# Unread products on TensorE in the planned gaps of the first two batches of a fused attention and FFN kernel

## The chip, the cores and the metric

The kernel runs on one core of a Trainium2 chip. The metric is the time of one execution on the device in microseconds (us), lower is better. The engines are named as in the profile: PE is TensorE (the matrix products; PEld its weight loads), DVE is VectorE, ACT is ScalarE, POOL is GpSimd, SP issues DMAs.

## The reference

Attention with a threshold on the scores is followed by a two-layer FFN. Each of 8 batches has 8 heads of 576 tokens by 64:

```python
scores = (1 / sqrt(64)) * q @ k.T
thresh = max(scores, axis=-1) - tau
scores = where(scores >= thresh, scores, -1e9)
attn = exp(scores - max(scores)); attn = attn / (sum(attn) + 1e-9)
x = (attn @ v)              # heads side by side: 4608 x 512
h = x @ w_in                # 512 x 2048
g = where(h >= 1, h, where(h <= -1, 0, (h + 1)**2 / 4))
out = g @ w_out             # 2048 x 512
```

## The kernel before, in words

Every large operand is split in a high and a low float16 part, so a product of two matrices is two or three products on PE. Heads go in pairs. A score tile is 128 queries by 576 keys of one head; its scores lie in one of two PSUM buffers, `s_ps[0]` and `s_ps[1]` (`s0` and `s1` of the pool `s`; in listings of the program `s_61` and `s_62`, in the profile both are `s`). Each buffer is two banks of 512 float32 columns, and the scores fill columns 0 to 287 of each bank.

A score tile goes through the engines like this: PE makes the scores (L806); DVE takes the row's maximum (L817 to L819); ACT takes the exponential (L822); DVE masks it and sums the row (L826, it reads the scores once more), then forms the divisor (L830, L831); POOL scales (L834), ACT makes the high part (L839), POOL the low part (L842), and a DMA transposes both (L845). PE multiplies by v (L924), ACT and DVE evict to x (L932, L936). The FFN's first product is L1000, its activation L1006 to L1023 on ACT and DVE, its second product L1049, the eviction L1068.

The first 130 us hold, beside the first batches, the preparation of the two weight matrices: they are loaded in 32 pieces, brought to float32 (L612 or L614, L621, L626, L630), measured by PE with `gram` (L637), scaled, and split (L682, L690, or PE's difference L702 and L703 with its eviction L709). v of the first batch is turned on PE (L526) in the buffers of the pool `s`.

No order is written by hand. `Plan.op` records each step with its engine, a cost in us, a key, what it comes after, and the buffers that it takes. `Plan.order` then plays the program through: each engine that is free takes the ready step of the lowest key, and the steps are emitted in the order in which they were started there; `o.t` is a step's start in the plan's own time. The keys are sums of tile numbers and fractions such as 19.77, 8.47 and 1.88. Every engine executes its steps strictly in the order emitted. Semaphore waits are put in from the tiles that the emitted instructions write and read.

## Time and profile before

| | us |
|---|---|
| median of 3 runs (1160.36 to 1167.64) | 1161.93 |
| profiled execution, its own time | 1162.28 |
| span in the profile | 1160.3 |
| PE busy | 1096.6 |
| DVE busy | 944.1 |
| ACT busy | 901.7 |
| POOL busy | 801.2 |

The profiled execution lies 0.35 us above the median, and 2.0 us of it lie outside the span. A row of a timeline begins with its start and its duration in us; then come engine, line, operation, result and operands, shape and count; in brackets stands how long the engine had been idle, and what released it. A row of the stretches (windows) has, for each engine, its busy us and its number of instructions, then the granted TensorE clock as a share of full speed.

### The profile page before, as it was taken

To read this page: it belongs to the slowest core of one execution; us is meant where nothing else is said; L and a number is where in the kernel's file an instruction comes from. 1 tells how busy PE (TensorE), PEld (TensorE's weight loads), DVE (VectorE), ACT (ScalarE), POOL (GpSimd) and SP (SyncE) were. 2 spreads that over 40 slices of the span, in tenths; PEclk is the share of its full clock that TensorE was granted. 3 is DMA by queue.
4 is the path that set the end of the run, shared out by engine and by line. 5 is a ranking of instruction groups with operands and counts; after the bars stand their busy time and mean duration, and the time that the engine had idled before them with its cause. 6 is when DMAs were issued, how large, how long until landed. Compare 5 with 4: busy or idle time off the path is not lost.

```text
span 1160.3 us, 27210 instructions
## 1 busy us (share of the span) xinstructions
PE 1096.6 (95%) x9423; PEld 755.4 (65%) x9423; DVE 944.1 (81%) x2982; ACT 901.7 (78%) x1692; POOL 801.2 (69%) x957
## 2 busy tenths in 40 slices
PE   5767989899999999999999999999999999999998
PEld 3335656776677567676677676676677677676674
DVE  5899778989889988888889987898889889786241
ACT  6998877887798779877878788877888788686362
POOL 3578997776976787667966887667966887654000
PEclk8889999999999999999999999999999999999999
DMA  8797999679995799668795899669995898555000
GB/s 328 287 228 138 160 208 193 123 156 172 181 175 108 138 196 212 126 114 189 171 180 92 169 205 185 137 105 196 175 179 101 165 186 166 99 102 92 19 2 28
DMA packets 435929, 179.40 MB, mean 155 GB/s; under 512 B 400464, under 2 KB 407632, under 8 KB 435792
## 3 DMA queue, kind: packets, MB, share of 16 engines
q1 hardware_dynamic: 435792, 177.67, 75.4%
q8 instruction: 74, 1.21, 0.4%
q14 instruction: 63, 0.52, 0.1%
HBM read 45.09 MB, written 9.44 MB: 47 GB/s over the span
## 4 chain that ended last, share of the span: by engine, by line
PE 48%; DVE 22%; POOL 10%; ACT 7%; issue 7%; DMA 5%; SPq 1%; ACTq 0%; POOLq 0%; DVEq 0%
PE acc L1049 18%; PE ph L1000 17%; PE s L806 6%; PE ph L924 5%; DVE sm L817 5%; DVE e L826 4%; POOL hl L842 3%; POOL e L834 2%; DVE ph L1013 2%; ACT e L822 2%; DMA eT<-hl 2%; ACT hl L839 2%; DVE vb L499 1%; POOL raw L415 1%; DVE sm L818 1%
## 5 line engine op out<-in xcount | busy, mean ns | idle before, releaser
L842 POOL TENSOR_TENSOR hl<-e,hl 128x576 f16<-128x576 f32 x286 | 368.1, 1292 | 121.2 <-ACT hl L839 118.8
L1000 PE MATMUL ph<-x,WI 128*128 128x256 f16 (+1 forms) x4032 | 402.1, 257 | 1.0 <-DVE x L936 0.5
L1000 PEld LDWEIGHTS <-WI 128*128 128x128 f16 x4032 | 347.1, 98 | 55.7 <-issue 4.1
L834 POOL TENSOR_SCALAR e<-e,sm 128x576 f32<-128x576 f32 x286 | 221.4, 779 | 98.8 <-DVE sm L831 63.9
L822 ACT ACTIVATE e<-s,sm,pc 128x576 f32<-128x576 f32 x288 | 237.3, 832 | 51.9 <-DVE sm L818 33.1
L826 DVE SCALAR_TENSOR_TENSOR e<-s,sm,e 128x576 f32<-128x576 f32 x288 | 231.1, 812 | 43.6 <-ACT e L822 39.2
L839 ACT ACTIVATE hl<-e 128x576 f16<-128x576 f32 x286 | 194.5, 683 | 64.2 <-POOL e L834 58.0
L817 DVE TENSOR_REDUCE sm<-s 128x1 f32<-128x576 f32 x288 | 215.5, 748 | 31.5 <-PE s L806 30.7
L1049 PE MATMUL acc<-WO,ga 128*128 128x512 f16 x864 | 206.7, 379 | 0.8 <-ACT ob L1068 0.8
L806 PE MATMUL s<-kk,qq 128*128 128x288 f16 (+3 forms) x1360 | 181.3, 290 | 16.9 <-DVE e L826 15.2
L806 PEld LDWEIGHTS <-qq 128*128 128x128 f16 (+3 forms) x1360 | 106.8, 100 | 78.5 <-issue 42.3
L1013 DVE SCALAR_TENSOR_TENSOR ph<-ph,fcs,asq 128x512 f32<-128x512 f32 (+1 forms) x160 | 111.8, 699 | 45.7 <-ACT asq L1009 44.7
L1006 ACT ACTIVATE asq<-ph,fcs 128x512 f32<-128x512 f32 (+1 forms) x160 | 116.2, 738 | 38.6 <-PE ph L1000 37.8
L1049 PEld LDWEIGHTS <-ga 128*128 128x128 f16 x864 | 81.9, 98 | 83.6 <-issue 4.7
L924 PE MATMUL ph<-eT,vst 128*64 128x320 f16 (+2 forms) x1928 | 126.5, 284 | 6.9 <-DVE gb L1023 3.1
L924 PEld LDWEIGHTS <-vst 128*64 128x64 f16 x1928 | 101.4, 111 | 30.4 <-issue 19.3
L1018 ACT ACTIVATE ga<-ph,fcs 128x256 f16<-128x256 f32 (+1 forms) x160 | 70.5, 451 | 33.5 <-DVE ph L1013 31.0
L1009 ACT ACTIVATE asq<-asq 128x512 f32<-128x512 f32 x144 | 90.8, 630 | 2.3
L1023 DVE SCALAR_TENSOR_TENSOR ga<-ph,fcs,ga 128x256 f16<-128x256 f32 (+1 forms) x160 | 70.8, 451 | 25.0 <-ACT gb L1018 9.4
L1049 PE MATMUL acc<-WO,gb 128*128 128x512 f16 x306 | 73.3, 379 | 0.0
L428 POOL TENSOR_TENSOR nat<-raw,nat 128x576 f16<-128x576 f32 x56 | 71.4, 1283 | 2.5 <-ACT nat L421 2.4
L818 DVE TENSOR_SCALAR sm<-sm,pc 128x1 f32<-128x1 f32 x288 | 61.7, 214 | 10.5
(162 smaller groups left out, 1210.2 us busy)
## 6 DMA issues: line engine op xcount, KB each, us to landing
kk<-nat SPq DMA_DIRECT2D x112, 144.0 KB, 3.3
raw<-in_v_dram SPq DMA_DIRECT2D x32, 288.0 KB, 3.7
raw<-in_q_dram SPq DMA_DIRECT2D x32, 288.0 KB, 3.6
raw<-in_k_dram SPq DMA_DIRECT2D x32, 288.0 KB, 3.6
WO<-in_moe_w_in_dram SPq DMA_DIRECT2D x16, 512.0 KB, 7.7
out_dram<-ob SPq DMA_DIRECT2D x32, 256.0 KB, 2.6
qq<-nat SPq DMA_DIRECT2D x112, 72.0 KB, 2.1
x<-in_moe_w_out_dram SPq DMA_DIRECT2D x10, 512.0 KB, 5.6
```

Of the source, the lines that this page charges most:

```text
L806: T.matmul(ap(x, s_ps)[r, f, :SH], q, k, start=ql == kl == 0, stop=kl == 1)
L817: V.tensor_reduce(t[:, 0:1], sv(), AX.XY, ALU.max, negate=True)
L822: A.activation(halves(ap(e, es)[:, :S]), sv(), AF.Exp, bias=ap(m, sm)[:, 1:2], scale=ap(cb, pc)[:, 24 + v : 25 + v])
L826: V.scalar_tensor_tensor(halves(ap(e, es)[:, :S]), sv(), t[:, 2:3], halves(ap(e, es)[:, :S]), ALU.is_ge, ALU.mult, accum_out=t[:, 3:4])
L834: G.tensor_scalar(ap(e, es)[:, :S], ap(e, es)[:, :S], ap(m, sm)[:, 5:6], 1.0, ALU.mult, ALU.mult)
L839: A.activation(ap(x, hl)[:, :S], ap(e, es)[:, :S], AF.Copy)
L842: G.tensor_tensor(ap(x, hl)[:, w : w + S], ap(e, es)[:, :S], ap(x, hl)[:, :S], ALU.subtract)
L924: T.matmul(o[hd * D : (hd + 1) * D, :n], vt[:, k, hd * D : (hd + 1) * D], t[:, kb, hd * n : (hd + 1) * n], start=m == 0, stop=m == len(blo ...
L1000: T.matmul(h[:, i], WTh["i"][:, u, wl * 512 + c * P : wl * 512 + (c + 1) * P], x[:, cc, xl, c0 : c0 + n].rearrange("p (t n) -> p t n", n=P ...
L1006: A.activation(tv()[:, :, c], hv()[:, :, c], AF.Relu, bias=fcs[:, b, 2, q : q + 1], scale=fcs[:, b, 1, q : q + 1])
L1013: V.scalar_tensor_tensor(hv()[:, :, c], hv()[:, :, c], fcs[:, b, 0, q : q + 1], tv()[:, :, c], ALU.max, ALU.min)
L1049: T.matmul(ap(ab, accs), gv(h, gl)[:, x], WTh["o"][:, fc + i, wl * 512 : (wl + 1) * 512], start=fc + i == 0 and m == 0, stop=fc + i == NFC ...
```

## The change

It has two parts.

**Unread products.** Where the steps are emitted, a PE step whose planned start lies over 0.8 us behind the planned end of the PE step before it, and before 240 us of the plan's time, gets products put just ahead of it: 0.65 of the planned gap, at 0.056 us for each product. Each is 128x128 by 128x128 of the constant `ones` (bfloat16), with a weight load of its own, and writes columns 384 to 511 of the second bank of `s_ps[0]`, which nothing reads. There are 593 of them in 27 groups, of 9 to 53 products. The first group stands ahead of everything else on PE.

**Keys.** Keys pass through `plan.key`, which adds nothing while `SHIFT` is empty, and are rounded to 3 decimals. Ties between sums of fractions then fall differently. The order of all real steps is the same as before up to the place that the trace of before has at about 366 us, and differs from there to the end.

```diff
+SHIFT = {}
+FILL = (0.8, 240, 0.65)
...
+    def key(self, kind, i, key):
+
+        return key + SHIFT.get(kind, {}).get(i, 0)
...
-        o = Op(eng, cost, key, fn, work)
+        o = Op(eng, cost, round(key, 3), fn, work)
...
+    def keep_warm(us):
+
+        for _ in range(int(us / 0.056)):
+            T.matmul(s_ps[0][:, 1, 512 - P :], ones, ones, start=True, stop=True)
+
     with tc.manual_schedule():
+        free = 5.0
         for o in plan.order():
+            if o.eng == "PE":
+                if FILL[0] < o.t - free and o.t < FILL[1]:
+                    keep_warm(FILL[2] * (o.t - free))
+                free = o.t + o.cost
             o.fn()
```

The other lines of the diff put `plan.key(...)` around keys that were passed bare.

First place: PE, where a piece of w_in is split (`dgw` is its scale, `ph` a PSUM buffer), in the trace of before at 76.43 us. Before:

```order
L637 LDWEIGHTS WO
L637 MATMUL acc<-WO 128x128
L702 MATMUL ph_64<-WI,dgw_132 128x512 [waits DVE_49]
L703 LDWEIGHTS minus
L703 MATMUL ph_64<-WI,minus 128x512 [waits Pool_49]
L637 LDWEIGHTS WO [waits DMAHW2_49,DVE_49,Activation_49]
L637 MATMUL acc<-WO 128x128
```

And now (23 products at the first place, 18 at the second, of which the first of each is shown; L646 is the old L637, L712 the old L702):

```order
L646 LDWEIGHTS WO
L646 MATMUL acc<-WO 128x128
L1096 LDWEIGHTS ones
L1096 MATMUL s_61<-ones 128x128 [waits DVE_49]
...
L712 MATMUL ph_64<-WI,dgw_132 128x512
L713 LDWEIGHTS minus
L713 MATMUL ph_64<-WI,minus 128x512 [waits Pool_49]
L646 LDWEIGHTS WO [waits DMAHW2_49,Activation_49]
L646 MATMUL acc<-WO 128x128
...
L1096 LDWEIGHTS ones
L1096 MATMUL s_61<-ones 128x128
```

The step L702 did not move against its neighbours, but a group stands ahead of it whose first product waits for a DVE instruction: by the semaphore's value, the mask (old L826) that is the last reader of the buffer `s_61` ahead of it in the program.

Second place: PE ahead of an FFN product L1049 (now L1062), in the trace of before at 167.30 us. Before:

```order
L702 MATMUL ph_63<-WO,dgw_134 128x512
L703 LDWEIGHTS minus
L703 MATMUL ph_63<-WO,minus 128x512 [waits Pool_49]
L1049 LDWEIGHTS ga_111
L1049 MATMUL acc<-WO,ga_111 128x512
```

Now, with 19 products, the first of which is shown:

```order
L712 MATMUL ph_63<-WO,dgw_134 128x512 [waits DVE_49]
L713 LDWEIGHTS minus
L713 MATMUL ph_63<-WO,minus 128x512 [waits Pool_49]
L1096 LDWEIGHTS ones
L1096 MATMUL s_61<-ones 128x128 [waits Activation_49]
...
L1062 LDWEIGHTS ga_111
L1062 MATMUL acc<-WO,ga_111 128x512
```

The FFN product, which uses no scores, now stands behind a wait for ACT: the exponential (old L822) that reads `s_61`.

Third place: DVE where the order first differs by the rounded keys, in the trace of before at about 367 us (`sm` holds a tile's row statistics, `scs` the scale of v). Before:

```order
L826 SCALAR_TENSOR_TENSOR e_92,sm_125<-s_62,sm_125,e_92 128x576
L830 TENSOR_SCALAR sm_125<-sm_125 128x1
L831 RECIPROCAL sm_125<-sm_125 128x1
L826 SCALAR_TENSOR_TENSOR e_93,sm_126<-s_61,sm_126,e_93 128x576
L481 TENSOR_REDUCE scs<-ph_65 128x1
```

Now:

```order
L837 SCALAR_TENSOR_TENSOR e_92,sm_125<-s_62,sm_125,e_92 128x576
L490 TENSOR_REDUCE scs<-ph_65 128x1
L302 TENSOR_SCALAR scs<-scs 128x1
L303 TENSOR_SCALAR scs<-scs 128x1
L304 TENSOR_SCALAR scs<-scs 128x1
L492 TENSOR_SCALAR scs<-scs 128x1
L841 TENSOR_SCALAR sm_125<-sm_125 128x1
L842 RECIPROCAL sm_125<-sm_125 128x1
L837 SCALAR_TENSOR_TENSOR e_93,sm_126<-s_61,sm_126,e_93 128x576
```

The scale of v moved ahead of a tile's divisor and the next tile's mask.

## The prediction

> **What bounds the kernel now.** I read the page first, then stretches by granted clock, then the chain of waits and the timelines of PE, DVE and ACT up to 207 us, where the change does most of its work.

> ```profile
> span 1160.3 us, 27210 instructions
> ...
> PEclk8889999999999999999999999999999999999999
> ```

> The second line is the granted clock in tenths over 40 slices of 29 us: it is reduced in the first four only. The stretches tell the two regimes apart (columns: PE, PEld, DVE, ACT, POOL busy us; clock; DMA share; GB/s):

> ```profile
> 0.00:207.21 207.21, 157.92 (x1497) 100.99 (x1498) 168.69 (x558) 169.76 (x324) 157.88 (x235) 0.93 0.90 217
> 22.89:29.72 6.83, 5.95 (x30) 2.63 (x31) 6.58 (x19) 5.64 (x10) 3.83 (x5) 0.50 0.88 306
> 43.37:50.20 6.83, 5.90 (x24) 2.45 (x21) 4.90 (x15) 6.30 (x14) 4.85 (x13) 0.50 0.75 242
> 149.19:152.60 3.41, 3.41 (x30) 2.55 (x27) 1.29 (x6) 1.73 (x5) 3.25 (x10) 0.50 1.07 286
> 207.21:210.63 3.42, 3.00 (x28) 2.74 (x27) 3.42 (x6) 3.20 (x6) 3.42 (x4) 0.50 0.45 86
> 362.00:1100.00 738.00, 730.03 (x6149) 508.10 (x6147) 618.98 (x1956) 576.54 (x1079) 523.53 (x593) 1.00 0.76 147
> ```

> From 362 us on PE is busy 730.03 of 738 us: PE carries that part, at full clock. Up to 207 us PE is busy 76%, DVE and ACT 81 and 82%: there the engines wait for each other in turn, and whatever is late at the end of it moves the whole PE part behind it. So the change is worth what it does to the arrival at 207 us, plus what the new order does after about 366 us. In this first part PE has 49 us of idle time and some stretches at half clock.

> **The gain: products that run at half clock today and lie on the chain of waits.** There are four such places.

> ```profile
> 9.97 5.33 PE L526 MATMUL s<-dgw,raw 128*128 128x128 f32 x20 [1.55 <-POOL dgw L514]
> ...
> 16.06 2.93 PE L526 MATMUL s<-dgw,raw 128*128 128x128 f32 x20
> ...
> 44.71 2.01 PE L702 MATMUL ph<-WI,dgw 128*128 128x512 f32 x2
> ...
> 47.95 2.08 PE L702 MATMUL ph<-WI,dgw 128*128 128x512 f32 x2 [0.29 <-DVE pc L402]
> ...
> 85.75 1.07 PE L702 MATMUL ph<-WI,dgw 128*128 128x512 f32 x2
> ...
> 129.71 2.23 PE L924 MATMUL ph<-eT,vst 128*64 128x320 f16 x30
> ...
> 148.65 3.73 PE L924 MATMUL ph<-eT,vst 128*64 128x320 f16 x30 [1.45 <-DMA eT<-hl]
> ```

> (a) The first turn of v takes 5.33 us, the second 2.93: at most 2.4 to win. Behind it the chain goes through loads:

> ```profile
> 26.80 6.33 DMA WO<-in_moe_w_in_dram
> 33.15 6.84 DMA x<-in_moe_w_out_dram
> ```

> The DMA engines are 88% taken in the stretch 22.89 to 29.72, so only 0.12 of 6.83 us is free to start loads earlier. I take 0.8 and keep 2.4 as the end. (b) Two differences L702 at half clock cost 2.01 and 2.08 against 1.07: 1.95. The group of 10 products between them finds no idle time in the trace and costs its own length, 0.6 at the pitch below; 1.4 is left. (c) L924 at 148.65 takes 3.73 against 2.23: 1.5; the group ahead of it, 16 products long, starts only when a mask on DVE releases its buffer:

> ```profile
> 148.27 0.81 DVE L826 SCALAR_TENSOR_TENSOR e<-s,sm,e 128x576 f32<-128x576 f32 x1
> ```

> That is 149.08, and with 0.9 for the group L924 is 1.3 late. I take zero for both together. (d) The half clock from 207.21 has no group ahead of it: zero. Together 2.2 us; the whole list without any lateness would be 5.9.

> [...]

> **The cost: groups that start late.** A group runs at the pitch of products with a load each:

> ```profile
> 92.01 2.84 PE L1000 MATMUL ph<-x,WI 128*128 128x128 f16 x48
> ```

> 2.84 / 48 = 0.059 us. 593 of them are 35 us, less than the 49 us of idle time. But the groups can't start when PE falls idle. They write into the first scores buffer, so each one waits for the last reader of that buffer ahead of it in the program (front, first and second place), and the real step stands behind it on PE. Where the gap came from that same reader, the whole group is added; where it came from elsewhere, the group adds a wait as well. [...]

> I price five groups in their own time frames: mask or exponential end, plus group, against the start of the next real step, and then the reader of what PE delivers late. They add up, since an earlier delay moves both sides.

> ```profile
> 64.30 0.81 DVE L826 SCALAR_TENSOR_TENSOR e<-s,sm,e 128x576 f32<-128x576 f32 x1
> ...
> 67.47 0.75 DVE L817 TENSOR_REDUCE sm<-s 128x1 f32<-128x576 f32 x1
> ...
> 76.88 0.81 DVE L826 SCALAR_TENSOR_TENSOR e<-s,sm,e 128x576 f32<-128x576 f32 x1
> ...
> 81.94 0.75 DVE L817 TENSOR_REDUCE sm<-s 128x1 f32<-128x576 f32 x1
> ...
> 91.83 0.81 DVE L826 SCALAR_TENSOR_TENSOR e<-s,sm,e 128x576 f32<-128x576 f32 x1
> ...
> 96.59 0.74 DVE L817 TENSOR_REDUCE sm<-s 128x1 f32<-128x576 f32 x1
> ```

> ```profile
> 65.17 0.40 PE L806 MATMUL s<-kk,qq 64*128 64x288 f16 x1 [3.06 <-DVE e L826]
> ...
> 76.43 1.13 PE L702 MATMUL ph<-WI,dgw 128*128 128x512 f32 x2 [1.64 <-DVE x L936]
> ...
> 77.61 0.39 PE L637 MATMUL acc<-WO 128*128 128x128 bf16 x4
> ...
> 79.34 1.13 PE L702 MATMUL ph<-WI,dgw 128*128 128x512 f32 x2 [1.34 <-ACT WI L709]
> ...
> 80.61 0.91 PE L806 MATMUL s<-kk,qq 64*128 64x288 f16 x12
> ...
> 91.76 0.41 PE L637 MATMUL acc<-WO 128*128 128x128 bf16 x4 [1.87 <-DVE WO L626]
> ...
> 94.78 0.91 PE L806 MATMUL s<-kk,qq 64*128 64x288 f16 x12
> ```

> - 65.17, 42 products (2.48): the mask ends at 65.11, the group at 67.59, the twelve score products 0.91 later at 68.50; DVE wants them at 67.47. Late by 1.0.
> - 76.43, 23 products (1.36), and 79.34, 18 products (1.06): the mask ends at 77.69, so L702 starts at 79.05. The work from 76.43 to 78.00 takes 1.57, the second group 1.06, so the second L702 starts at 81.68, 2.3 late, and the scores of 80.61 end at 83.9; DVE wants them at 81.94. Late by 1.9.
> - 91.76, 26 products (1.53): mask end 92.64, group end 94.17, 2.4 late; the scores of 94.78 end at 98.1, DVE wants them at 96.59. Late by 1.5.

> ```profile
> 113.24 1.10 PE L702 MATMUL ph<-WO,dgw 128*128 128x512 f32 x2 [3.24 <-DVE ph L295]
> ...
> 167.30 1.46 PE L1049 MATMUL acc<-WO,ga 128*128 128x512 f16 x6
> ...
> 176.33 1.17 PE L806 MATMUL s<-kk,qq 128*128 128x288 f16 x8
> ```

> ```profile
> 113.68 0.81 DVE L826 SCALAR_TENSOR_TENSOR e<-s,sm,e 128x576 f32<-128x576 f32 x1
> ...
> 116.43 0.76 DVE L817 TENSOR_REDUCE sm<-s 128x1 f32<-128x576 f32 x1 [0.47 <-PE s L806]
> ...
> 177.68 0.74 DVE L817 TENSOR_REDUCE sm<-s 128x1 f32<-128x576 f32 x1
> ```

> ```profile
> 168.29 1.55 ACT L822 ACTIVATE e<-s,sm,pc 128x576 f32<-128x576 f32 x2
> ```

> - 113.24, 28 products (1.65): mask end 114.49, group end 116.14. Late by 2.9, and DVE waits for PE already at 116.43.
> - 167.30, 19 products (1.12): the exponentials end at 169.84, the group at 170.96, L1049 is 3.7 late. PE has no gap from there on, so the scores of 176.33 are 3.7 late too. The first four of the eight products (0.6) end at 180.6; DVE wants them at 177.68. Late by 2.9.

> The sum is 10.2 us. Four more groups behind 80 us (13, 17, 26 and 17 products, 4.3 us) are left out of it, some of their lateness will be hidden, and they go into the upper end. The remaining groups I cost at nothing: they fall into idle time that is long enough, or into the loads' time before 40 us; if that cover is gone, each costs its length. So the first part ends 10.2 - 2.2 = 8.0 us later.

> **The order from 366 us.** The same steps, other neighbours. PE idles 738 - 730.03 = 8.0 us there, so 8 us is the most that a better order can win; a worse one could lose as much again (an estimate: the idle time doubled). No row speaks for a side, so zero, with 8 either way.

> The sum: 1162.28 + 8.0 = 1170.3 for the profiled execution; it stands 0.35 above the median, so 1170.

> **Rivals.** *The clock wins (not slower).* PE's lateness falls into slack on DVE and ACT, and the groups clear the half-clock stretches. For it: 49 us of idle time on PE, and four slow products on the chain. Against it: DVE's rows at 67.47 and 81.94 follow without idle time. It gives 1161.9 - 5.9 = 1156, up to 1162 with part of the lateness. Half of PE's busy time in the stretches up to 152.60 (5.95, 5.90 and 3.41) would be 7.6 us, of which the chain has those 5.9. *The groups themselves run at half clock.* The two longest groups in the middle of this part have 42 products each, and the second of them follows an idle time of 3.06 us (row 65.17); at twice 0.059 both together cost 84 x 0.059 = 5.0 us more: 1175. *The new order is worse:* 8 us on top, 1178; or better by 8, 1162. *The change does nothing:* the groups are in the program, so this only remains as a balance of gain and cost; it is inside the first rival.

> **How the numbers follow.** My forecast, 1164 to 1176, has 0.43; the clock wins 0.20; groups at half clock 0.13; a worse order 0.15, a better one 0.09. Changes under 1%, 1150.3 to 1173.6, count as within. Slower by over 1%: the worse order, most of the half clock and a fifth of the forecast, 0.37. Faster by over 1% needs the whole clock gain and a good order at once: 0.04. Within: 0.59. For 8 in 10 the range goes from the clock's end, 1156, to the worse order with some of the unpriced groups, 1181.

> **What would show it.** The L526 at about 10 us at 2.9, and the L702 at 45 to 50 us at 1.1, would show the gain; weight loads and L637 around them tell how much the loads swallow. The step L1049 of 167.30 should come some 10 us later than before, directly behind a group that waits for ACT, and PE should reach full load around 215 instead of 207. If that step comes earlier than 167 the cost is wrong. PE's idle time from there to 1100 us tells the new order: 8 us as before, or more. A granted clock of 0.5 inside the groups would show the second rival.

## The result and the profile after

| | before | after |
|---|---|---|
| median, six runs each, us | 1162.67 (1160.36 to 1167.64) | 1179.76 (1175.68 to 1181.57) |
| ratio, 95% interval | | 1.014 [1.0117, 1.0162] |
| profiled execution, its own time / span | 1162.28 / 1160.3 | 1179.6 / 1177.8 |

The changed kernel is 17.1 us slower, where the forecast had 8. Its 1179.76 lies above the forecast's 1164 to 1176. Lines after the change stand 9 to 13 higher: L526 is L535 now, L702 is L712, L806 is L817, L817 is L828, L822 is L833, L826 is L837, L924 is L935 and L1049 is L1062. The products are L1096.

These are lines of the page of after: span, granted clock by slices, the group of DVE's row maxima, and the group of the products. The second fence is the maxima's group on the page of before.

```profile
span 1177.8 us, 28431 instructions
PEclk9999999999999999999999999999999999999999
L828 DVE TENSOR_REDUCE sm<-s 128x1 f32<-128x576 f32 x288 | 215.6, 749 | 58.4 <-PE s L817 57.6
L1096 PE MATMUL s<-ones 128*128 128x128 bf16 x593 | 43.6, 238 | 31.5 <-DVE e L837 21.7
```

```profile
L817 DVE TENSOR_REDUCE sm<-s 128x1 f32<-128x576 f32 x288 | 215.5, 748 | 31.5 <-PE s L806 30.7
```

The clock went up: no slice is at 8 any more. The place where the time went is DVE's maxima: 58.4 us of idle time ahead of them instead of 31.5, nearly all of it waiting for scores. And 21.7 us of PE's idle time now ends with the mask (L837), in front of a product. The view of that one line tells what the products waited for (us, times) and who waited for them:

```profile
its engine sat idle before it (us, times) until:
...
  DVE e L837: 21.7, 10
...
  ACT e L833: 4.4, 3
...
who waited for it (us, times):
  DVE e L837: 1.7, 2
  ACT e L833: 1.4, 1
```

Ten groups waited for a mask and three for the exponential: the wait that the prediction describes. It had not thought of the last two lines: three times DVE or ACT, whose next steps read the same buffer, waited for the group itself.

The stretches by clock (columns as in the prediction), of after, and two of them of before:

```profile
7.28:55.07 47.79, 38.03 (x420) 27.59 (x418) 39.64 (x126) 42.56 (x86) 22.96 (x47) 1.00 0.92 345
55.07:58.48 3.41, 3.41 (x35) 2.87 (x34) 3.41 (x11) 3.16 (x6) 3.27 (x4) 0.50 0.41 126
116.51:123.33 6.82, 5.69 (x39) 3.91 (x40) 2.45 (x13) 2.24 (x5) 1.67 (x3) 0.50 0.48 91
174.53:177.95 3.42, 2.90 (x27) 2.90 (x27) 2.06 (x6) 0.90 (x3) 2.78 (x4) 0.50 0.99 155
184.77:188.19 3.42, 3.42 (x10) 1.22 (x9) 1.23 (x6) 0.63 (x2) 2.88 (x4) 0.50 0.00 0
384.00:1118.00 734.00, 725.59 (x6108) 503.93 (x6106) 617.67 (x1945) 576.96 (x1071) 518.37 (x591) 1.00 0.77 148
```

```profile
7.28:55.07 47.79, 34.10 (x220) 20.43 (x220) 37.77 (x118) 40.37 (x82) 21.76 (x44) 0.86 0.91 343
366.00:1100.00 734.00, 726.03 (x6100) 504.91 (x6098) 615.05 (x1945) 573.52 (x1071) 520.35 (x591) 1.00 0.77 148
```

Up to 55 us the granted clock rose from 0.86 to 1.00. Behind that, half clock stands at four places on or right behind a late group; a fifth, 225.73 to 229.15, is the one that before has at 207.21. Around 10 us the views show 1.00, in after from its first clock record at 7.28 us on, in before (9.24 to 16.06) ahead of its first one at 16.07, so that the first turn of v ran at half clock there is read from its length alone, 5.33 us against 2.93 for the same products. In the 734 us from 384 on PE idles 8.4 us, in the same length of before 8.0.

To see where the time went, I took the start of the same DVE row in both timelines (DVE's order is the same up to 366 us) and noted by how much the later kernel is behind. Most steps between such rows are terms of the prediction's sum; the places are in the time of before.

| between these starts in before, us | what lies there | forecast | measured |
|---|---|---|---|
| 0 to 21.35 | first turn of v | -0.8 | -1.9 |
| 21.35 to 53.17 | two L702 | -1.4 | -1.3 |
| 53.17 to 56.47 | masks that wait for ACT, ahead of the first group of 42 | nothing | +1.2 |
| 56.47 to 69.42 | 65.17, second group of 42, and the first behind 55.87 | +1.0 | +1.1 |
| 69.42 to 84.21 | 76.43 and 79.34, 23 and 18 | +1.9 | +1.8 |
| 84.21 to 95.79 | 13 products | left out | +0.6 |
| 95.79 to 113.41 | 91.76, 26, and a group of 17 | +1.5 | +1.5 |
| 113.41 to 117.22 | 113.24, 28 | +2.9 | +5.6 |
| 117.22 to 149.12 | smaller groups | left out | +1.6 |
| 149.12 to 164.05 | L924 and its group | 0 | -0.2 |
| 164.05 to 168.56 | 164.01, 26 | left out | +3.5 |
| 168.56 to 194.86 | 167.30, 19 | +2.9 | +3.7 |
| 194.86 to 364.14 | the last groups | nothing | +1.0 |
| 364.14 to the end | the order | 0 | -0.7 |
| sum | | +8.0 | +17.5 |

The 1.2 from 53.17 to 56.47 is not the price of the group of 42. The first of the two masks there, at 54.98 in before without a wait, waits 1.26 us for the exponential on ACT; it ends before the group begins at 53.95, and in first_ten (below), which has no group at this place, it waits just as long. DVE's rows of after, and then of first_ten:

```profile
53.08 0.82 DVE L837 SCALAR_TENSOR_TENSOR e<-s,sm,e 128x576 f32<-128x576 f32 x1 [1.26 <-ACT e L833]
```

```profile
52.55 0.82 DVE L837 SCALAR_TENSOR_TENSOR e<-s,sm,e 128x576 f32<-128x576 f32 x1 [1.26 <-ACT e L833]
```

This exponential starts 1.9 us earlier in after than in before (52.21 against 54.12), DVE's row at 53.17 by 3.1: what DVE was ahead of ACT is lost here.

The other rows behind the table, PE's timeline of after (start, duration, then the row as before; in brackets the idle time ahead and its releaser):

```profile
10.04 2.97 PE L535 MATMUL s<-dgw,raw 128*128 128x128 f32 x20 [0.25 <-POOL dgw L523]
...
42.72 1.08 PE L712 MATMUL ph<-WI,dgw 128*128 128x512 f32 x2
...
45.59 1.13 PE L712 MATMUL ph<-WI,dgw 128*128 128x512 f32 x2
...
53.95 3.65 PE L1096 MATMUL s<-ones 128*128 128x128 bf16 x42 [2.45 <-DVE e L837]
...
63.28 2.50 PE L1096 MATMUL s<-ones 128*128 128x128 bf16 x42 [2.70 <-DVE e L837]
...
117.64 3.15 PE L1096 MATMUL s<-ones 128*128 128x128 bf16 x28 [4.23 <-DVE e L837]
...
120.58 2.02 PE L712 MATMUL ph<-WO,dgw 128*128 128x512 f32 x2
...
175.05 2.93 PE L1096 MATMUL s<-ones 128*128 128x128 bf16 x26 [3.03 <-DVE e L837]
...
183.41 1.22 PE L1096 MATMUL s<-ones 128*128 128x128 bf16 x19 [2.13 <-ACT e L833]
...
184.46 2.45 PE L1062 MATMUL acc<-WO,ga 128*128 128x512 f16 x6
...
186.71 2.19 PE L1062 MATMUL acc<-WO,gb 128*128 128x512 f16 x6
```

And what DVE does behind the three dearest groups, in DVE's timeline of after:

```profile
125.07 0.76 DVE L828 TENSOR_REDUCE sm<-s 128x1 f32<-128x576 f32 x1 [6.02 <-PE s L817]
...
180.04 0.76 DVE L828 TENSOR_REDUCE sm<-s 128x1 f32<-128x576 f32 x1 [3.42 <-PE s L817]
...
184.73 0.82 DVE L837 SCALAR_TENSOR_TENSOR e<-s,sm,e 128x576 f32<-128x576 f32 x1 [1.24 <-PE s L1096]
...
189.82 0.76 DVE L828 TENSOR_REDUCE sm<-s 128x1 f32<-128x576 f32 x1 [3.75 <-PE s L817]
```

The first of these maxima stands in before at 116.43 with 0.47 us of waiting (quoted in the prediction). The second and the fourth have no idle time ahead of them there:

```profile
166.49 0.75 DVE L817 TENSOR_REDUCE sm<-s 128x1 f32<-128x576 f32 x1
...
171.14 0.74 DVE L817 TENSOR_REDUCE sm<-s 128x1 f32<-128x576 f32 x1
```

So the products hold PE, PE delivers scores late, and DVE stands still for 6.02, 3.42 and 3.75 us where it stood for 0.47, 0 and 0.

### The profile page after: what moved, and what is told of

It reads as the page before. It is cut to its first block, busy times and chain, and to the rows that moved or that the text cites. A ratio compares the mean times of both kernels' runs of the same rounds, so it can differ in the third digit from the quotient of the medians.

```text
span 1177.8 us, 28431 instructions
## 1 busy us (share of the span) xinstructions
PE 1123.5 (95%) x10016; PEld 786.4 (67%) x10016; DVE 947.8 (80%) x2982; ACT 906.1 (77%) x1692; POOL 799.4 (68%) x957
## 4 chain that ended last, share of the span: by engine, by line
PE 72%; DVE 14%; ACT 5%; issue 3%; DMA 2%; POOL 2%; SPq 0%; ACTq 0%; DVEq 0%; POOLq 0%
PE acc L1062 26%; PE ph L1013 26%; PE s L817 10%; PE ph L935 8%; DVE sm L828 3%; DVE e L837 3%; PE s L1096 2%; DVE ph L1026 1%; ACT e L833 1%; DVE ga L1036 1%; DMA raw<-in_v_dram 1%; DVE sm L829 1%; POOL hl L853 1%; DVE gb L1036 1%; DMA x<-in_moe_w_out_dram 1%
## 5 line engine op out<-in xcount | busy, mean ns | idle before, releaser
L845 POOL TENSOR_SCALAR e<-e,sm 128x576 f32<-128x576 f32 x286 | 216.8, 762 | 110.1 <-DVE sm L842 72.6
L833 ACT ACTIVATE e<-s,sm,pc 128x576 f32<-128x576 f32 x288 | 237.1, 831 | 55.0 <-DVE sm L829 35.4
L828 DVE TENSOR_REDUCE sm<-s 128x1 f32<-128x576 f32 x288 | 215.6, 749 | 58.4 <-PE s L817 57.6
L837 DVE SCALAR_TENSOR_TENSOR e<-s,sm,e 128x576 f32<-128x576 f32 x288 | 231.8, 812 | 33.5 <-ACT e L833 25.4
L1062 PE MATMUL acc<-WO,ga 128*128 128x512 f16 x864 | 206.8, 380 | 1.1 <-ACT ob L1082 0.8
L817 PE MATMUL s<-kk,qq 128*128 128x288 f16 (+3 forms) x1360 | 177.4, 288 | 7.0 <-DVE e L837 6.9
L817 PEld LDWEIGHTS <-qq 128*128 128x128 f16 (+3 forms) x1360 | 105.8, 100 | 66.4 <-issue 28.9
L1062 PEld LDWEIGHTS <-ga 128*128 128x128 f16 x864 | 81.8, 98 | 84.1 <-issue 4.5
L935 PE MATMUL ph<-eT,vst 128*64 128x320 f16 (+2 forms) x1928 | 125.2, 282 | 3.1 <-DVE gb L1036 2.5
L935 PEld LDWEIGHTS <-vst 128*64 128x64 f16 x1928 | 98.9, 111 | 26.7 <-issue 16.7
L1036 DVE SCALAR_TENSOR_TENSOR ga<-ph,fcs,ga 128x256 f16<-128x256 f32 (+1 forms) x160 | 70.7, 450 | 17.3 <-ACT WO L1031 6.3
L1062 PE MATMUL acc<-WO,gb 128*128 128x512 f16 x306 | 74.2, 382 | 0.0
L1096 PE MATMUL s<-ones 128*128 128x128 bf16 x593 | 43.6, 238 | 31.5 <-DVE e L837 21.7
```

The source lines that it names most:

```text
L817: T.matmul(ap(x, s_ps)[r, f, :SH], q, k, start=ql == kl == 0, stop=kl == 1)
L828: V.tensor_reduce(t[:, 0:1], sv(), AX.XY, ALU.max, negate=True)
L833: A.activation(halves(ap(e, es)[:, :S]), sv(), AF.Exp, bias=ap(m, sm)[:, 1:2], scale=ap(cb, pc)[:, 24 + v : 25 + v])
L837: V.scalar_tensor_tensor(halves(ap(e, es)[:, :S]), sv(), t[:, 2:3], halves(ap(e, es)[:, :S]), ALU.is_ge, ALU.mult, accum_out=t[:, 3:4])
L845: G.tensor_scalar(ap(e, es)[:, :S], ap(e, es)[:, :S], ap(m, sm)[:, 5:6], 1.0, ALU.mult, ALU.mult)
L935: T.matmul(o[hd * D : (hd + 1) * D, :n], vt[:, k, hd * D : (hd + 1) * D], t[:, kb, hd * n : (hd + 1) * n], start=m == 0, stop=m == len(blo ...
```

## The experiments

Theory W says that the loss is the wait: a group holds PE until the last reader of the scores buffer has come. Rival O says that the new order behind 366 us is most of it. Later runs ask whether a group costs by its wait or by its length, and what a single group costs alone. All kernels are built on the changed one, with a counter `g` of the groups. The unread products that they leave out change no output.

**One: the order alone, and each half of the groups.** The first ten groups, 9 to 53 products each, run up to 44 us.

```diff
-        free = 5.0
+        free, g = 5.0, 0
...
-                    keep_warm(FILL[2] * (o.t - free))
+                    g += 1
+                    pass            # keys_only
+                    # first_ten:   if g <= 10: keep_warm(...)
+                    # from_eleven: if g > 10:  keep_warm(...)
+                    # one_each:    keep_warm(FILL[2] * (o.t - free) if g <= 10 else 0.06)
```

keys_only, no products at all:

> Theory W (a group waits for the last reader of the scores buffer and then holds PE; the new order costs nothing): the change without any unread products is the time of before within 2 us, 1161 to 1164, since in the changed kernel's trace the lateness is 18.2 us at the place where the order starts to differ and 17.5 us at the end. Rival O (the rounded keys cost as much as the products): 1167 or more.

first_ten:

> Leaves out the unread products behind the first ten groups, so up to about 50 us all is as in the changed kernel. Theory W: the 3.1 us by which DVE is ahead at 50 us are kept to the end: 1159 to 1161. Rival S (an early lead is swallowed later by loads and by the slack of the engines): 1162 to 1164.

from_eleven:

> Only the groups from the eleventh on. Theory W: the changed kernel's loss behind 50 us, 18.2 + 3.1 = 21 us, on top of before: 1180 to 1186. Rival: the first ten groups set up part of the loss (another phase of the clock, other neighbours), and without them the loss is under 15 us: under 1178.

one_each, the first ten groups whole and a single product for each later one:

> The first ten groups whole, and of each later group one product alone, with the wait that it has. If the wait alone holds PE up, worked out from the trace of before (end of the reader against the start of the next real step, less the slack of who reads it): 5 to 7 us lost behind the 3 us won, 1164 to 1167. If only the length of the groups counts, nothing is lost: 1159 to 1161. If the wait were nearly all of it (late start and half clock), 1172 or more.

| kernel | us (lowest to highest), runs | ratio to before, 95% |
|---|---|---|
| before, in these runs | 1162.73, 19 | |
| keys_only | 1166.03 (1164.13 to 1169.79), 10 | 1.0029 [1.0014, 1.0043] |
| first_ten | 1162.39 (1161.68 to 1164.57), 10 | 0.9996 [0.9986, 1.0007] |
| one_each | 1173.83 (1171.66 to 1176.10), 4 | 1.0094 [1.0071, 1.0117] |
| after | 1179.76, 6 | 1.014 [1.0117, 1.0162] |
| from_eleven | 1185.02 (1182.54 to 1189.47), 4 | 1.019 [1.0155, 1.0225] |

The order alone costs 1166.03 - 1162.73 = 3.3 us, between what either theory expected: it is a part of the loss, and not its bulk. The first ten groups win 1166.03 - 1162.39 = 3.6 against the same order without them. (1162.39 as such lies where Rival S was expected, because Theory W had counted nothing for the order.) The seventeen later ones lose 1185.02 - 1166.03 = 19.0 without the first ten, which puts from_eleven where Theory W had it, and 1179.76 - 1162.39 = 17.4 with them. Of these 17.4 a single product in the place of each group already costs 1173.83 - 1162.39 = 11.4, more than the 5 to 7 expected of the wait alone, and in the range put down for a wait that also brings half clock (1172 or more): so two thirds are the wait, with the half clock that came with it (one_each has half clock at 115.72, 153.26, 170.33 and 177.16), and the length of the groups is the other 5.9.

The lag behind before at the same DVE rows (the table above, in us) shows the same place by place:

| start in before, us | keys_only | first_ten | one_each | after | from_eleven |
|---|---|---|---|---|---|
| 53.17 | 0.0 | -3.6 | -3.7 | -3.1 | -0.4 |
| 113.41 | 0.4 | -1.8 | 0.9 | 3.1 | 7.9 |
| 117.22 | 1.9 | -0.5 | 3.8 | 8.6 | 13.4 |
| 194.86 | 0.0 | -2.0 | 9.9 | 17.3 | 22.0 |
| 364.14 | 0.3 | -2.1 | 10.1 | 18.2 | 23.0 |
| end | 3.6 | 0.6 | 10.4 | 17.5 | 24.8 |

Of the lead that first_ten has over keys_only, 3.6 at 53.17, 2.4 is left at 364 and 3.0 at the end; so a part of it is swallowed, as Rival S has it. keys_only is level with before again at 364 (0.3) and loses its 3.3 behind that: the order is to blame, in this run. In after the same stretch came out 0.7 better than in before. The difference goes with the clock, which in keys_only falls once there (stretches of keys_only, the second right behind the first):

```profile
558.78:562.19 3.41, 1.45 (x10) 0.67 (x9) 3.41 (x6) 1.31 (x4) 3.41 (x5) 1.00 1.06 199
562.19:565.60 3.41, 3.41 (x13) 1.21 (x13) 3.15 (x14) 2.05 (x4) 3.24 (x8) 0.50 1.13 229
...
366.00:1100.00 734.00, 724.23 (x6087) 502.24 (x6085) 617.01 (x1942) 573.94 (x1067) 518.05 (x591) 1.00 0.75 148
```

PE idles 9.8 us in 734 here, against 8.0 in before. All ten profiles with the new order can be compared so. Eight have one such piece of half clock between 560 and 850 us, and they lose 1.8 to 3.7 us from 364 to the end against before (those of the later experiments are counted in). The two without, after and one_each, come out at -0.7 and +0.3. So the cost of the new order goes with such a piece, which most of its runs have and some have not. The piece can't be all of the cost: half clock for 3.41 us (0.50 in the second row) takes at most 1.7 us of PE's work, an estimate from these rows. What the rest is, is not shown. PE was busy 1.45 us in the first row; how often half clock came behind such a piece is counted in the last section.

**Two: the same products into another buffer.** If the wait is for the scores buffer, the same products into a buffer that the next PE step takes anyway, or that is free, must lose less. In ph_target a later group goes into a buffer of the pool `ph`; the plan notes which are free. Groups 11, 12, 19 and 27 are left out, because no such buffer was free there or the next step takes a scores buffer. s_target leaves out the same four and keeps the scores buffer as the target: it is the control.

```diff
-                pick.t = now
+                pick.t, pick.spare = now, list(self.free["ph"])
...
-    def keep_warm(us):
+    def keep_warm(us, i=None):
+        t = s_ps[0][:, 1, 512 - P :] if i is None else ph[i][:, 512 - P :]
...
+                    mine = [b.slot for b in o.take if b.pool == "ph"] + o.spare
+                    if g <= 10:
+                        keep_warm(FILL[2] * (o.t - free))
+                    elif mine and not any(b.pool == "s" for b in o.take):
+                        keep_warm(FILL[2] * (o.t - free), mine[0])   # s_target: without mine[0]
```

s_target:

> Control for the next run: the changed kernel without the four later groups whose next step takes a scores buffer (the eleventh, twelfth, nineteenth and twenty-seventh); all others write where they did, in the first scores buffer. By the changed kernel's trace these four cost 1.2 + 1.1 + 0 + 0.8 = 3.1 us: 1175 to 1178.

ph_target:

> The same groups of the same length in the same places; the later ones write into the PSUM buffer that the next step takes anyway, or into one that the plan has free, so that they no longer wait for readers of scores. Theory W (the foreign wait is most of the loss behind the first ten groups): 5 to 9 us less than the control, 1167 to 1171; what stays is the groups whose gap was itself a wait for that buffer, which are then added in their own length (76.43, 79.34 and 113.24 us, together about 4 us) and those that found no gap. Rival L (PE's time itself is what is lost): as the control, within 2 us.

s_target: 1179.99 (1178.30 to 1181.60, four runs), ratio 1.0138 [1.0115, 1.0161]: above the 1175 to 1178 expected, which had counted the 1.2 of the masks as the price of a group. At 69.42 it is 2.5 ahead of before, where after is 0.8 ahead; but its clock is at half from 76.03 to 79.44, where after has full clock, and at 84.21 it is 1.3 behind against 1.0. At 364 us it is 15.8 behind against 18.2 in after, and it then lost 3.3 us, with a piece of half clock at 577.79, where after had won 0.7. ph_target: 1169.6 (1168.97 to 1170.86, four runs), ratio 1.0054 [1.0036, 1.0072], inside Theory W's 1167 to 1171: 10.4 us less than s_target, with the same number of products, where 5 to 9 were expected. Three of the groups in PE's timeline, of s_target, and then of ph_target:

```profile
75.75 2.39 PE L1097 MATMUL s<-ones 128*128 128x128 bf16 x23 [2.48 <-DVE e L837]
...
94.56 1.61 PE L1097 MATMUL s<-ones 128*128 128x128 bf16 x26 [2.44 <-DVE e L837]
...
117.93 3.15 PE L1097 MATMUL s<-ones 128*128 128x128 bf16 x28 [4.54 <-DVE e L837]
```

```profile
74.76 2.61 PE L1097 MATMUL ph<-ones 128*128 128x128 bf16 x23 [2.15 <-DVE x L947]
...
92.63 1.61 PE L1097 MATMUL ph<-ones 128*128 128x128 bf16 x26 [1.76 <-DVE WO L635]
...
115.27 2.81 PE L1097 MATMUL ph<-ones 128*128 128x128 bf16 x28 [3.14 <-DVE gb L1036]
```

PE waits 0.3, 0.7 and 1.4 us less ahead of them, and another step on DVE releases them: it is the buffer and not the number of products that makes the larger part. Even so ph_target stays 7.2 us above first_ten (1169.6 - 1162.39, on another chip, where before has 1163.2 instead of 1162.73). In the rows shown its groups still start late, after 1.76 to 3.14 us of waiting: about when the gap that they should fill is over.

**Three: single groups.** Each of these kernels has the new order and one group alone: number 20 (28 products, at 113.24), number 25 (26 products, at 164.01, left out of the sum), number 26 (19 products, at 167.30).

```diff
+                    g += 1
+                    if g == 20:      # 25, 26
+                        keep_warm(FILL[2] * (o.t - free))
```

> One group alone, the one of 28 products ahead of the step that was at 113.24 us. My prediction priced it at 2.9; in the changed kernel DVE fell back by 5.6 at that place, with the clock at half. If the group's own wait makes the clock fall, 5 to 6 us again, with a half-clock stretch on it; if the fall came from the groups before it, 3 us and full clock.

> One group alone, the one of 26 products ahead of the step that was at 164.01 us, which the prediction left out of its sum. By the prediction's way of pricing (mask end 164.95, 1.53 for the group, against 164.01; then 2.4 until DVE's next maximum at 166.49 has its scores) DVE falls back by 2.1 there. The changed kernel showed 3.5, with the clock at half on the group. If the price of 3.5 is the group's own, 3.5 again; if the half clock is a matter of where the clock's window falls, about 2.

> One group alone, the one of 19 products ahead of the FFN product that was at 167.30 us. The prediction: 2.9. The changed kernel showed 3.7 from the exponentials to the next batch's start (13.55 to 17.25), with a peak of 5.2 and the clock at half behind the group. If its price is a held PE with no gap behind it, 2.5 to 4.5 between DVE's rows of 168 and 195 us; if it was the half clock, under 2 where the clock stays up.

One execution each, so these are readings of the timelines: 1168.86, 1167.70 and 1170.04 us. PE's rows at the place, of only_20, only_25 and only_26 in turn:

```profile
114.67 2.73 PE L1097 MATMUL s<-ones 128*128 128x128 bf16 x28 [4.54 <-DVE e L837]
```

```profile
165.14 2.46 PE L1097 MATMUL s<-ones 128*128 128x128 bf16 x26 [3.23 <-DVE e L837]
```

```profile
171.99 1.58 PE L1097 MATMUL s<-ones 128*128 128x128 bf16 x19 [2.13 <-ACT e L833]
...
173.36 2.77 PE L1062 MATMUL acc<-WO,ga 128*128 128x512 f16 x6
```

Number 20 puts DVE back by 4.5 us (from 0.1 to 4.6 at the rows 113.41 and 117.22), between the two values expected, with half clock from 115.16 to 118.58. keys_only loses 1.5 between the same rows with no group, and only_25 and only_26 1.5 and 1.6, all three with a stretch at half clock there. So the group's own price is some 3.0, and the forecast's 2.9 for it was sound; what it lacked is the half clock. Number 25 costs 3.8 at its place (0.1 to 3.9), of which 2.6 is left at 194.86: it should not have been left out. It has half clock there again (165.69 to 169.10). only_26 has it at the same place (165.86 to 169.27) without this group, and falls back by 0.6 only (0.8 to 1.4); so the larger part of the 3.8 is the group's. Number 26 costs 4.4 by 194.86 (1.4 to 5.8), against the forecast's 2.9. It is not shown whether that is the held PE: the clock fell to half behind the group here too (172.69 to 176.10, the first L1062 at 2.77 instead of 1.46), so the run does not tell the two expected readings apart.

**Four: the first ten groups with the old order.** The two good halves together: the keys as they were, and the first ten groups.

```diff
-        o = Op(eng, cost, round(key, 3), fn, work)
+        o = Op(eng, cost, key, fn, work)
...
+                    if g <= 10:
+                        keep_warm(FILL[2] * (o.t - free))
```

> The first ten groups alone, with keys that are not rounded, so in the order of before. If the two parts add up (first ten groups 3.6 us less, new order 3.3 us more), 1158 to 1160. Rival: the order's price was the runs' spread, and the gain is then smaller too: 1161 to 1163.

1157.8 us (1155.72 to 1159.96, six runs) against 1163.2 of before in eleven runs on the same chip, ratio 0.995 [0.9933, 0.9967], just below the 1158 to 1160 expected if the parts add up: this version beats both kernels, by 5.4 us over before. By the medians above, the early gain is 3.6 of it. In this profile, however, the lead is 1.4 at 364 us and 5.0 at the end. PE idles 5.1 us in the 734 from 364, where before has 8.0; why the same order of instructions waited less there stays open.

## Why the prediction was right and wrong

**The mechanism held.** Groups wait for the last reader of the scores buffer (21.7 us of PE's idle time behind masks, 4.4 behind exponentials), PE then comes late, and DVE's maxima pass it on (58.4 us of idle time instead of 31.5). Two runs show it: one product in the place of each later group costs 11.4 of 17.4 us, and the same products in another buffer 10.4 less. The terms whose groups ran at full clock came out as worked: forecast 1.0, measured 1.1 (65.17, with the first group of 42 in the same step); forecast 1.9, measured 1.8 (76.43 and 79.34); forecast 1.5, measured 1.5 (91.76).

**The gain was read too small at one point.** Step (a) took 0.8 of 2.4, with the loads as the limit; measured is 1.9, and the lead is still there at 53 us, so the loads swallowed little; it is the masks behind 53 us, waiting for ACT, that took 1.2 of it. Step (b) was right: forecast 1.4, measured 1.3. The rival "the clock wins" is true for the first ten groups alone: they win 3.6 us by the medians. Its 7.6 us was worked out with two stretches missing: before is at half clock also from 57.03 to 60.44 and from 63.85 to 70.68, with 3.40 and 5.17 us of work on PE, which would make it 11.9. That a group ahead of a slow step brings the clock up was an assumption of the author's, in these steps and in this rival. Up to 55 us the clock did go up (0.86 in before and keys_only, 1.00 in after); behind that half clock stands on or behind four groups (55.07, 116.51, 174.53, 184.77).

**The step that failed is the sum of the costs: 10.2 forecast, 21.3 measured up to 364 us.** 13.7 of it belongs to the five priced places, 7.6 to what was left out. First, "four more groups are left out of it": the one of 26 products at 164.01 costs 3.5, and by the very method that priced the others (mask end 164.95 from the row 164.13 below, plus 1.53, against L702 at 164.01, less some slack on DVE) it would have had some 2. The rest, 4.1, is 1.2 of lost lead at 53 us and 2.9 for the other groups left out or costed at nothing. Second, "A group runs at the pitch of products with a load each", a pitch taken at full clock: the groups at 113.24 and 164.01 and the steps behind those at 113.24 and 167.30 ran at half clock. At 113.24 the group took 3.15 instead of 1.65 and the two L712 2.02 instead of 1.10: 2.4 us, and 2.9 + 2.4 = 5.3 against the 5.6 measured. At 164.01 the group took 2.93 instead of 1.53. At 167.30 the two L1062 took 4.64 instead of 2.92; the lag rose by 5.2 at its highest and 3.7 of it stayed. The mask at 184.73, waiting 1.24 for the group, was in no step. The two rows of before for the group left out, DVE's and PE's:

```profile
164.13 0.82 DVE L826 SCALAR_TENSOR_TENSOR e<-s,sm,e 128x576 f32<-128x576 f32 x1
```

```profile
164.01 1.12 PE L702 MATMUL ph<-WO,dgw 128*128 128x512 f32 x2 [2.03 <-DVE sm L830]
```

**"Groups at half clock"** was a rival with 5.0 us, all for the two groups of 42. Of these the first did run slowly (3.65 instead of 2.48, behind 2.45 us of idle time; what that cost is not seen apart), the second did not (2.50, behind 2.70 us). That groups can run at half clock was right, the place was wrong: it fell on later groups (3.15 instead of 1.65, 2.93 instead of 1.53).

**The order** was put at zero within 8 us either way. It costs 3.3 by the medians of keys_only, inside these ends. The profile of after shows -0.7, by luck: no piece of half clock fell behind 364 us in it, as it did in eight of the ten profiles with this order.

**What would show it.** L535 at 2.97 and the L712 at 42.72 and 45.59 at 1.08 and 1.13 came as foretold; the step of 167.30 came at 184.46, 17 us later and not some 10, behind a group that waits for ACT. L924 at 207.62, where PE's full load begins in before, came at 225.69 instead of the forecast's 215 or so. PE's idle time in 734 us of that part stayed at 8 (8.4).

## What to carry to other kernels

A product that nobody reads is still a step of its queue: here ten groups waited for a mask and three for an exponential that read the buffer which they write (21.7 and 4.4 us of PE's idle time), and the real steps behind them waited with them. Fill gaps only where the target is free when the gap begins, here the first 44 us, and test the fill apart from any change of order that comes with it. When such lateness is priced, leave no group out of the sum because it is small, and price each at full and at half clock (28 products: 1.65 us priced, 3.15 measured at half clock).

## What the runs showed of the hardware

From 10 to some 1145 us, half clock came in pieces of 3.41 us, one or two together, in every profile, and the starts of the pieces of one run lie on one grid of 3.413 us. In before the starts 43.37, 57.03, 63.85, 149.19 and 207.21 lie 6, 10, 12, 37 and 54 such lengths behind 22.89: (207.21 - 22.89) / 54 = 3.413. Its first line lies at 2.41 us in before and keys_only, at 0.46 in after and at 3.08 in one_each. Cutting all twelve profiles along their own grids, I counted by PE's busy time what follows a full-clock piece (the pieces ahead of the first clock record, which lies at 16.07 us in before, count as full):

| PE busy in the piece of 3.41 us | next piece at half clock | next piece at full clock |
|---|---|---|
| under 1.35 us | 68 | 0 |
| 1.35 to 1.9 us | 19 | 32 |
| over 1.9 us | 0 | 3748 |

This was the hidden luck in the profile of before. The same place in before and in keys_only, on grids that lie alike, in the view of stretches, before first:

```profile
111.64:115.05 3.41, 1.81 (x23) 0.97 (x25) 3.31 (x13) 3.41 (x6) 3.41 (x5) 1.00 0.51 96
115.05:118.47 3.42, 3.42 (x51) 2.37 (x46) 2.12 (x12) 3.42 (x8) 3.03 (x5) 1.00 0.77 122
```

```profile
111.64:115.05 3.41, 1.37 (x7) 0.53 (x9) 3.31 (x14) 3.41 (x6) 3.41 (x5) 1.00 0.45 84
115.05:118.47 3.42, 3.42 (x43) 2.55 (x42) 1.44 (x9) 3.04 (x7) 3.02 (x4) 0.50 0.73 113
```

The order of instructions is the same here, and PE was busy 1.81 us in the one and 1.37 in the other: full clock in the one and half in the other. Eleven of the twelve profiles have half clock at this place, five of them with no group there at all; before is the only one without. The full clock at 113.24, from which the forecast took its durations, was the exception. It is not in the time of before, though: keys_only, 1.9 behind at 117.22, is level again at 194.86. Whether the longer wait makes the drop there surer can't be told from runs that nearly all have it.
